# Expert blocks with their weight conversions in another order: one behind each eviction, five behind the last, and the cast of the scatter's indices behind the last eviction

## The chip, the cores and the metric

The kernel runs on one core of a Trainium2 chip. Such a core has five engines that each work through a list of their own: TensorE (PE, matmuls), VectorE (DVE), ScalarE (ACT), GpSimd (POOL) and SyncE (SP, which here issues nearly all transfers). What is compared is the device time of one execution in microseconds (us). Each profile is one execution, with a time stamp for every instruction.

## The reference

Three stages follow each other: attention masked by cluster, a feed-forward layer with a softmax gate on its hidden values, and a layer of eight experts in which each token goes to one expert. The change touches the last stage alone:

```python
expert_idx = np.argmax(logits, axis=1)          # N = 1536 tokens, E = 8 experts, capacity = 384
# token i goes to row pos[i] of expert expert_idx[i], in order, as long as rows are free
h = np.maximum(np.einsum('ecd,edf->ecf', disp, w1), 0.0)    # D = 512, F = 1024
y = np.einsum('ecf,efd->ecd', h, w2)
out[i] = gate_w[i] * y[expert_idx[i], pos[i]]               # zero where no row was free
```

The weights `w1` and `w2` come as 32-bit numbers, 4 MB per expert.

## The kernel before, in words

**How an expert is computed.** Every 32-bit operand is split into two 16-bit numbers, a high part and a low part, and a product is made of three matmuls (high x high, high x low, low x high). For the weights, ScalarE converts to the high part (`ah` for `w1`, `bh` for `w2`, L990) and VectorE computes the low part from the 32-bit number and the high part (`al`, `bl`, L991). An expert's weights come in eight pieces of 0.5 MB: 0 to 3 are `w1`, 4 to 7 are `w2`. SP loads each piece into a staging buffer (`w`, L987) of which the stage has eight, and each buffer can be loaded again when VectorE's conversion has read it.

**A block.** `block(e)` records the work of expert e on its first 256 tokens (in block 0, on its second 128 tokens). The first product (`gemm1`, L1065 to L1067) fills four banks of PSUM with the hidden values, 24 matmuls each. Each bank is evicted by two instructions: ScalarE writes the high part `hh` (L1078) and VectorE the low part `hl` (L1079), which reads `hh` too. Then the second product (`gemm2`, L1084 to L1086) runs through the hidden values once for each 128 tokens, 24 matmuls of 512 columns each; every third one (L1086) reads `hl`. ScalarE scales the result (`yo`, L1089), and GpSimd scatters it to the tokens' rows in DRAM (L1092). The row numbers of the scatter come with the tokens: SP loads them as 32-bit floats (`idf`, L1036) and VectorE casts them to integers (`ids`, L1042). Where an expert has more than 256 tokens, a branch runs `extra` for the rest; this part stands in the program between the first matmuls of the next block.

**What a block does for later ones.** While block e computes, it loads the tokens of expert e + 1 (`cxT`, L1032, and `idf`) and eight pieces of weights: 2 to 7 of expert e + 2 and 0 and 1 of expert e + 3. It converts the eight pieces that the block before has loaded: 2 to 7 of expert e + 1 and 0 and 1 of expert e + 2.

**What sets the order.** Each block is planned by itself. `add` takes for each step its engine, a cost, a due time `at`, and the keys that it reads and writes. `order` sorts the steps by `at` and derives the dependences from the keys in that order; `emit` then plays the steps through on a model of the engines and issues them in the order in which they start there. In the expert stage the due time weighs most in the choice (`MIX` is 0.1). The times of this model are those of the planner and not of the chip; only the order that results goes into the program. The waits between the engines are put in from the real buffers, so a planner's dependence that is missing or one too many changes an order and nothing else.

In the kernel before, the pieces' conversions are due at 5.0, 7.0, 9.0 and so on, two steps (ScalarE's and VectorE's) of a piece together, and none is held back beyond the first eviction (key `("hh", b, 0)`). The cast `ids` is due right behind its load (`at + 0.02`).

Of the kernel before, what the change touches and what calls it, by code (L numbers as in the profile page):

```python
# [25 lines left out]
CAP = 384  # L26
P = 128
# [3 lines left out]
KC, FC = DM // P, DF // P  # L31
# [42 lines left out]
class Plan:  # L74
# [12 lines left out]
    def add(self, eng, cost, at, fn, reads=(), writes=(), data=0.0, lead=1e9, get=None, put=None):  # L87
        if put is not None:
            put.puts += 1
        self.todo.append((eng, cost, at, fn, tuple(reads), tuple(writes), data, lead, get, put))  # L90
# [906 lines left out]
def c_piece(nc, plan, piece, e, i, at, later=None):  # L997

    n = 8 * e + i
    j = n % 3 if n < FIRST else 3 + (n - FIRST) % LATE  # L1000
    cost = dict(sp=0.6, act=0.95, dve=1.14)

    def conv(eng, f, at, reads=()):
        plan.add(eng, cost[eng], at, f, reads=[("cst", j), *reads], writes=[("cw", e, i)])

    def run(eng, f):
        if eng == "sp":
            plan.add(eng, cost[eng], at, f, reads=["turn"], writes=[("cst", j)], data=0.52)
        elif later is None:
            conv(eng, f, at + 6)  # L1010
        else:
            later.append(lambda at, reads: conv(eng, f, at, reads))

    piece(e, i, run)


class Experts:
# [23 lines left out]
        s = slice(a // P, b // P)  # L1041
        self.nc.vector.tensor_copy(out=self.X[e][2][:, s], in_=self.X[e][1][:, s])  # L1042

    def xload(self, e, at, parts):
        add = self.plan.add

        def rows(a, b):
            if e not in self.X:
                self.X[e] = self.tiles(self.xk, e, CAP) if e >= 0 else self.tiles(self.pools["cx0"], e, P)
            self.rows(e, a, b)  # L1050

        for a, b in parts:
            k = (e % 2, b)
            add("sp", 2.7 * (b - a) / CAP, at, lambda a=a, b=b: rows(a, b), reads=["xs", "turn"], writes=[("cxT", k)], data=0.97 * (b - a) / CAP)
        for a, b in parts:
            k = (e % 2, b)
            add("sp", 0.65, at + 0.01, lambda a=a, b=b: self.idf(e, a, b), reads=["xs", ("cxT", k)], writes=[("idf", k)], data=0.06)
            add("dve", 0.07, at + 0.02, lambda a=a, b=b: self.ids(e, a, b), reads=[("idf", k)], writes=[("ids", k)])

    def gemm1(self, o, e, f, j, nb):  # L1060
        nc, w, x = self.nc, self.W[max(e, 0)], self.X[e][0]
# [34 lines left out]
    def block(self, e, start):  # L1096
        add, plan = self.plan.add, self.plan
        b = e % 2
        j0, nb = (1, 1) if e == 0 else (0, 2)
        per = 4 // nb  # L1100
        t = 2.0
        if e == 0:
            self.xload(0, 0.0, [(P, 2 * P), (2 * P, CAP)])
        if e + 1 < E:
            self.xload(e + 1, 1.5, [(0, CAP)])
        last, self.later = self.later, []
        for n, f in enumerate(last):
            f(5.0 + 2.0 * (n // 2), [("hh", b, 0)])
        for n, i in enumerate(range(8 * e + start, min(8 * e + start + 8, 8 * E))):
            c_piece(self.nc, plan, self.piece, i // 8, i % 8, 6.0 + 2.0 * n if e else 1.6 + 0.1 * n, self.later)  # L1110
        kx = [("cxT", (b, 2 * P if e == 0 else CAP))]
        for n in range(FC // per):
            k = Hold()
            for f in range(per):
                def g1(k=k, f=f, n=n):
                    if not (n or f):
                        self.hidden(e, nb)
                    self.gemm1(k.bank[:, f * nb * P : (f + 1) * nb * P], e, per * n + f, j0, nb)

                add("pe", 0.645 * nb, t, g1, reads=kx + [("cw", e, i) for i in range(4)], writes=[k], get=None if f else k)  # L1120
                t += 0.645 * nb
            add("act", 0.48, t, lambda k=k, n=n: self.evac(k.bank, e, n, nb)[0](), reads=[k], writes=[("hh", b, n)])
            add("dve", 0.6, t + 0.01, lambda k=k, n=n: self.evac(k.bank, e, n, nb)[1](),
                reads=[k, ("hh", b, n)], writes=[("hl", b, n)], put=k)
        for i in range(nb):
            k = Hold()
            for f in range(FC):
                add("pe", 0.645, t + 0.02, lambda f=f, k=k, i=i: self.gemm2(k.bank, e, f, i),
                    reads=[("hh", b, f // per), ("hl", b, f // per), ("cw", e, 4 + f // 2)], writes=[k], get=None if f else k)
                t += 0.645  # L1130
            add("act", 0.48, t + 0.02, lambda k=k, i=i: self.scale(k.bank, i), reads=[k], writes=[("yo", i)], put=k)
            add("pool", 1.0, t + 0.03, lambda i=i: self.put(e, j0 + i, i),
                reads=[("yo", i), ("ids", (b, 2 * P if e == 0 else CAP))], data=0.26)
        plan.emit()
# [192 lines left out]
```

## Time and profile before

| | |
|---|---|
| median of three runs | 578.1 us (576.29 to 578.87) |
| the profiled execution | 578.46 us |
| its span in the profile | 576.7 us |
| TensorE busy | 502.8 us (87%) |
| VectorE busy | 414.8 us (72%) |
| ScalarE busy | 365.2 us (63%) |
| GpSimd busy | 276.9 us (48%) |

The expert stage begins at about 396 us. The busy share of an engine is a mean over stages of which each has its own limit, so what a stage is limited by is read from the waits in that stage. A matmul's recorded duration is longer than the time until the next one can start; distances from start to start say more than durations. The third part of expert 2 (`extra`) is run here, inside block 3; in the other blocks the branch is passed over.

### The profile page before, as it was taken

What the parts mean: (1) busy time and instruction counts of PE and PEld (TensorE: products, weight loads), DVE (VectorE), ACT (ScalarE), POOL (GpSimd) and SP (SyncE); (2) the same over time, 40 slices, a digit from 0 to 9 for tenths busy, and PEclk for the clock granted to TensorE, in tenths of its full rate; (3) what the DMA queues carried; (4) which work ended last, traced back from release to release, by engine and by line L of the source; (5) the groups of instructions that cost most, each with busy time, mean ns of one, the idle gap of its engine ahead of it and who ended that gap; (6) DMA issues with size and microseconds to landing.
All of it is one profiled execution on the core that took longest, in us unless ns stands there. A gap on an engine that the chain in (4) does not pass through costs nothing. (4 is left out here: it accounts for less than half of the span.)

```text
span 576.7 us, 13094 instructions
## 1 busy us (share of the span) xinstructions
PE 502.8 (87%) x4945; PEld 325.5 (56%) x4945; DVE 414.8 (72%) x976; ACT 365.2 (63%) x553; POOL 276.9 (48%) x292
## 2 busy tenths in 40 slices
PE   1578898878788888997988999998989999999996
PEld 1356676656565554654554444465746775675672
DVE  7699999999989899997655999961436253753610
ACT  3576897988677898996845889831616162562420
POOL 2167798999978767888742444520000101001001
PEclk9967998999889999999999999999999999999999
DMA  8898777796878799999999687958988456984300
GB/s 247 237 186 226 243 204 215 209 289 158 180 188 184 171 206 156 209 221 196 209 194 237 184 198 196 270 126 178 324 304 233 162 141 234 298 219 160 73 9 17
DMA packets 159340, 113.75 MB, mean 197 GB/s; under 512 B 126560, under 2 KB 135074, under 8 KB 159268
## 3 DMA queue, kind: packets, MB, share of 16 engines
q1 hardware_dynamic: 156660, 106.31, 76.2%
q0 software_dynamic: 2320, 6.32, 3.1%
q8 instruction: 46, 0.75, 0.5%
q14 instruction: 26, 0.21, 0.1%
q10 hardware_dynamic: 288, 0.16, 0.1%
HBM read 51.57 MB, written 17.11 MB: 119 GB/s over the span
## 5 line engine op out<-in xcount | busy, mean ns | idle before, releaser
L408 POOL TENSOR_TENSOR pr<-pf,pr 128x384 f16<-128x384 f32 x168 | 173.6, 1063 | 52.5 <-ACT pr L460 26.2
L1092 POOL DMA_INDIRECT out_dram<-yo,ids x16 | 16.0, 1000 | 160.5 <-ACT yo L1089 131.8
L1065 PE MATMUL psb<-cxT,ah 128*128 128x256 f16 (+1 forms) x288 | 71.8, 261 | 1.7 <-DMA cxT<-xs 1.7
L1067 PE MATMUL psb<-cxT,al 128*128 128x256 f16 (+1 forms) x288 | 71.9, 261 | 0.9 <-PEq L1168 0.3
L1066 PE MATMUL psb<-cxT,ah 128*128 128x256 f16 (+1 forms) x288 | 71.8, 261 | 0.0
L502 DVE TENSOR_REDUCE mm<-psb 128x1 f32<-128x384 f32 x132 | 67.0, 545 | 4.9 <-PE psb L499 4.3
L1079 DVE SCALAR_TENSOR_TENSOR hl<-psb,hh 128x512 f16<-128x512 f32 x32 | 21.8, 685 | 67.2 <-ACT hh L1078 41.8
L536 PE MATMUL psS<-QK 96*128 96x384 f32 x132 | 61.2, 498 | 0.0
L499 PE MATMUL psb<-QK 96*128 96x384 f32 x132 | 46.9, 418 | 14.6 <-DVE mm L502 7.5
L544 ACT ACTIVATE pf<-psS 128x768 f32<-128x768 f32 x66 | 53.2, 806 | 9.5 <-PE psS L536 6.3
L1089 ACT ACTIVATE yo<-psb 128x512 f32<-128x512 f32 x17 | 10.1, 597 | 77.4 <-PE psb L1086 50.0
L544 ACT ACTIVATE pr<-psS 128x768 f16<-128x768 f32 x66 | 52.6, 803 | 8.7 <-PE psS L536 8.5
L1086 PE MATMUL psb<-bh,hl 128*128 128x512 f16 x128 | 48.6, 380 | 4.9 <-DVE hl L1079 4.9
L1084 PE MATMUL psb<-bh,hh 128*128 128x512 f16 x128 | 48.5, 379 | 0.0
L1085 PE MATMUL psb<-bl,hh 128*128 128x512 f16 x128 | 48.5, 379 | 0.0
L535 PE MATMUL psS<-QK 128*128 128x384 f16 x132 | 46.1, 349 | 1.6 <-ACT pr L544 1.0
L557 PE MATMUL psb<-V,pr 128*128 128x65 f16 x396 | 43.7, 196 | 3.9 <-DVE mm L502 3.6
L991 DVE SCALAR_TENSOR_TENSOR al<-w,ah 128x1024 f16<-128x1024 f32 x32 | 38.9, 1244 | 8.2 <-ACT ah L990 8.2
L559 PE MATMUL psb<-V,pr 128*128 128x65 f16 x396 | 43.4, 194 | 1.1 <-POOL pr L408 1.1
L558 PE MATMUL psb<-V,pr 128*128 128x64 f16 x396 | 43.4, 198 | 0.0
L557 PEld LDWEIGHTS <-pr 128*128 128x128 f16 x396 | 37.3, 98 | 7.4 <-issue 2.6
L558 PEld LDWEIGHTS <-pr 128*128 128x128 f16 x396 | 37.7, 99 | 5.4 <-issue 4.4
(193 smaller groups left out, 1561.2 us busy)
## 6 DMA issues: line engine op xcount, KB each, us to landing
w<-in_w_dram SPq DMA_DIRECT2D x64, 512.0 KB
xs<-X SPq DMA_DIRECT2D x12, 516.0 KB
QK<-hr SPq DMA_DIRECT2D x16, 384.0 KB
QK<-hl SPq DMA_DIRECT2D x32, 192.0 KB
x<-in_qkT_dram SPq DMA_DIRECT2D x7, 768.0 KB
lT<-in_w_in_dram SPq DMA_DIRECT2D x8, 512.0 KB
lT<-in_w_out_dram SPq DMA_DIRECT2D x8, 512.0 KB
v<-in_vP_dram SPq DMA_DIRECT2D x8, 384.0 KB
```

Of the source, the lines that this page charges most:

```text
L408: nc.gpsimd.tensor_tensor(out=out[:, i], in0=a[:, i], in1=b[:, i], op=ALU.subtract)
L502: add("dve", 0.465, at(c - 9.9 + 0.25 * g), lambda c=c, g=g, w=w: nc.vector.tensor_reduce(out=m2[mm][:, c, g : g + 1], in_=w.bank[:, :384] ...
L536: nc.tensor.matmul(o, k1[:, ks], q1[:, qs], start=False, stop=True)
L544: add("act", 0.691, at(k + 0.5), lambda dst=dst, kb=kb: nc.scalar.activation(dst, ps[kb][:, :, :384], AF.Exp, scale=SC), reads=[kb], write ...
L557: nc.tensor.matmul(A, ph[ub][:, c, qs], v[:, j, c, 0:65], start=(c == 0), stop=False)
L558: nc.tensor.matmul(A[:, :64], ph[ub][:, c, qs], v[:, j, c, 65:129], start=False, stop=False)
L1065: nc.tensor.matmul(o, w["ah"][:, c, fs], x[:, 0, c, ts], start=(c == 0), stop=False)
L1066: nc.tensor.matmul(o, w["ah"][:, c, fs], x[:, 1, c, ts], start=False, stop=False)
L1067: nc.tensor.matmul(o, w["al"][:, c, fs], x[:, 0, c, ts], start=False, stop=(c == KC - 1))
L1084: nc.tensor.matmul(y, hh[:, f, i], w["bh"][:, f], start=(f == 0), stop=False)
L1085: nc.tensor.matmul(y, hh[:, f, i], w["bl"][:, f], start=False, stop=False)
L1086: nc.tensor.matmul(y, hl[:, f, i], w["bh"][:, f], start=False, stop=(f == FC - 1))
```

## The change

It gives other due times and other keys to two kinds of steps; no instruction is added or removed.

- The k-th piece's conversion (k from 0) is now due and held behind the eviction of bank g = min(k, 3) (in block 0, which has two banks: min(k, 1)): the first conversion behind the first eviction, the second behind the second, the third behind the third, and the other five behind the fourth.
- The cast `ids` is now due behind the block's last bank and is held behind that bank's `hh` (the last one: `FC // per - 1`).

```diff
-    def xload(self, e, at, parts):
+    def xload(self, e, at, parts, late=()):
...
-            add("dve", 0.07, at + 0.02, lambda a=a, b=b: self.ids(e, a, b), reads=[("idf", k)], writes=[("ids", k)])
+            add("dve", 0.07, late[0] if late else at + 0.02, lambda a=a, b=b: self.ids(e, a, b), reads=[("idf", k), *late[1:]], writes=[("ids", k)])
...
+        late = (2.4 + 0.645 * nb * FC, ("hh", b, FC // per - 1))
         if e == 0:
-            self.xload(0, 0.0, [(P, 2 * P), (2 * P, CAP)])
+            self.xload(0, 0.0, [(P, 2 * P), (2 * P, CAP)], late)
         if e + 1 < E:
-            self.xload(e + 1, 1.5, [(0, CAP)])
+            self.xload(e + 1, 1.5, [(0, CAP)], late)
         last, self.later = self.later, []
         for n, f in enumerate(last):
-            f(5.0 + 2.0 * (n // 2), [("hh", b, 0)])
+            g = min(n // 2, FC // per - 1)
+            f(2.3 + 0.645 * nb * per * (g + 1) + 1.2 * (n // 2 - g), [("hh", b, g)])
```

The program up to the expert stage is the same instruction for instruction. TensorE's list is the same throughout. On VectorE the list of block 1 reads as follows before; `hl_1` is an eviction, `al` and `bl` are conversions with the piece's number in `w_2` to `w_7`, and `ids` is the cast.

```order
L1079 SCALAR_TENSOR_TENSOR hl_1_6336<-psb_4711,hh_1_6335 128x512
L991 SCALAR_TENSOR_TENSOR al_5453<-w_2_6097,ah_5452 128x1024
L991 SCALAR_TENSOR_TENSOR al_5453<-w_3_6112,ah_5452 128x1024
L991 SCALAR_TENSOR_TENSOR bl_5455<-w_4_6127,bh_5454 128x1024
L1079 SCALAR_TENSOR_TENSOR hl_1_6336<-psb_75,hh_1_6335 128x512
L991 SCALAR_TENSOR_TENSOR bl_5455<-w_5_6141,bh_5454 128x1024
L1079 SCALAR_TENSOR_TENSOR hl_1_6336<-psb_73,hh_1_6335 128x512
L991 SCALAR_TENSOR_TENSOR bl_5455<-w_6_6155,bh_5454 128x1024
L1042 CAST ids_6351<-idf_6350 128x3
L991 SCALAR_TENSOR_TENSOR bl_5455<-w_7_6168,bh_5454 128x1024
L1079 SCALAR_TENSOR_TENSOR hl_1_6336<-psb_4710,hh_1_6335 128x512
```

Six conversions and the cast stand ahead of the last eviction. In the changed kernel the same stretch reads:

```order
L1079 SCALAR_TENSOR_TENSOR hl_1_6336<-psb_4711,hh_1_6335 128x512
L991 SCALAR_TENSOR_TENSOR al_5453<-w_2_6097,ah_5452 128x1024
L1079 SCALAR_TENSOR_TENSOR hl_1_6336<-psb_75,hh_1_6335 128x512
L991 SCALAR_TENSOR_TENSOR al_5453<-w_3_6112,ah_5452 128x1024
L1079 SCALAR_TENSOR_TENSOR hl_1_6336<-psb_73,hh_1_6335 128x512
L991 SCALAR_TENSOR_TENSOR bl_5455<-w_4_6127,bh_5454 128x1024
L1079 SCALAR_TENSOR_TENSOR hl_1_6336<-psb_4710,hh_1_6335 128x512
L1042 CAST ids_6351<-idf_6350 128x3
L991 SCALAR_TENSOR_TENSOR bl_5455<-w_5_6141,bh_5454 128x1024
L991 SCALAR_TENSOR_TENSOR bl_5455<-w_6_6155,bh_5454 128x1024
L991 SCALAR_TENSOR_TENSOR bl_5455<-w_7_6166,bh_5454 128x1024
```

Three conversions stand ahead of the last eviction, the cast behind it, and five conversions behind the cast. ScalarE's list moves in the same way: `hh` and a conversion in turn, and behind the fourth `hh` five conversions, then the scaling of the outputs. On SP, before, the list of block 2 begins so; `cxT` and `idf` are the tokens and the row numbers of expert 3, and `w_2` to `w_6` the pieces of expert 4.

```order
L1032 DMA_TRANSPOSE cxT_6687<-xs 128x8x384
L987 DMA w_2_6746<-in_w_dram 128x1024
L987 DMA w_3_6763<-in_w_dram 128x1024
L1036 DMA idf_6688<-xs 128x3x1
L987 DMA w_4_6780<-in_w_dram 128x2x512
L987 DMA w_5_6798<-in_w_dram 128x2x512
L987 DMA w_6_6812<-in_w_dram 128x2x512
```

And in the changed kernel:

```order
L1032 DMA_TRANSPOSE cxT_6687<-xs 128x8x384
L987 DMA w_4_6715<-in_w_dram 128x2x512
L987 DMA w_5_6718<-in_w_dram 128x2x512
L987 DMA w_2_6748<-in_w_dram 128x1024
L1036 DMA idf_6688<-xs 128x3x1
L987 DMA w_3_6779<-in_w_dram 128x1024
L987 DMA w_6_6827<-in_w_dram 128x2x512
```

Pieces 4 and 5 have moved ahead of 2 and 3, and `idf` stands behind three loads instead of two. In both kernels the k-th load of a block takes the buffer that the k-th conversion of the block frees, and waits for that conversion on VectorE. The fourth load (`w_3`) so waits for the fourth conversion, which in the changed kernel stands behind the cast, and the cast waits for `idf`.

## Rows read from the trace of the kernel before

**Rows 1.** The page: TensorE's busy time, and the chain that ended last.

```profile
PE 502.8 (87%) x4945; PEld 325.5 (56%) x4945; DVE 414.8 (72%) x976; ACT 365.2 (63%) x553; POOL 276.9 (48%) x292
...
issue 7%; DMA 3%; DVE 0%; ACT 0%; POOLq 0%; POOL 0%
```

**Rows 2.** TensorE's waits from 390 us: us in total, times, longest.

```profile
PE psb L1086 <- DVE hl L1079: 4.9, 4, 2.4
PE psb L1065 <- DMA cxT<-xs: 1.7, 1, 1.7
```

**Rows 3.** Timeline of TensorE: start us, us, engine, line, operation, count, [idle before].

```profile
421.76 0.38 PE L1085 MATMUL psb<-bl,hh 128*128 128x512 f16 x1
424.58 0.39 PE L1086 MATMUL psb<-bh,hl 128*128 128x512 f16 x1 [2.44 <-DVE hl L1079]
...
447.34 0.39 PE L1086 MATMUL psb<-bh,hl 128*128 128x512 f16 x1 [1.43 <-DVE hl L1079]
...
479.47 0.39 PE L1086 MATMUL psb<-bh,hl 128*128 128x512 f16 x1 [0.58 <-DVE hl L1079]
...
500.42 0.38 PE L1085 MATMUL psb<-bl,hh 128*128 128x512 f16 x1
500.82 0.39 PE L1086 MATMUL psb<-bh,hl 128*128 128x512 f16 x1
...
522.58 0.39 PE L1086 MATMUL psb<-bh,hl 128*128 128x512 f16 x1 [0.43 <-DVE hl L1079]
```

**Rows 4.** Timeline of ScalarE, blocks 1, 2, 6 and 7.

```profile
409.69 0.60 ACT L1078 ACTIVATE hh<-psb 128x512 f16<-128x512 f32 x1 [2.02 <-PE psb L1067]
410.41 2.00 ACT L990 ACTIVATE ah<-w 128x1024 f16<-128x1024 f32 x2
412.32 1.04 ACT L990 ACTIVATE bh<-w 128x1024 f16<-128x1024 f32 x1
...
433.45 0.60 ACT L1078 ACTIVATE hh<-psb 128x512 f16<-128x512 f32 x1 [2.02 <-PE psb L1067]
...
531.46 0.60 ACT L1078 ACTIVATE hh<-psb 128x512 f16<-128x512 f32 x1 [1.97 <-PE psb L1067]
...
552.61 0.60 ACT L1078 ACTIVATE hh<-psb 128x512 f16<-128x512 f32 x1 [1.97 <-PE psb L1067]
...
560.78 0.60 ACT L1078 ACTIVATE hh<-psb 128x512 f16<-128x512 f32 x1 [2.02 <-PE psb L1067]
566.01 0.60 ACT L1089 ACTIVATE yo<-psb 128x512 f32<-128x512 f32 x1 [4.63 <-PE psb L1086]
```

**Rows 5.** Timeline of VectorE, block 1.

```profile
411.88 0.69 DVE L1079 SCALAR_TENSOR_TENSOR hl<-psb,hh 128x512 f16<-128x512 f32 x1 [0.58 <-DVEq L1168]
412.49 2.35 DVE L991 SCALAR_TENSOR_TENSOR al<-w,ah 128x1024 f16<-128x1024 f32 x2
414.76 1.22 DVE L991 SCALAR_TENSOR_TENSOR bl<-w,bh 128x1024 f16<-128x1024 f32 x1
...
418.23 1.21 DVE L991 SCALAR_TENSOR_TENSOR bl<-w,bh 128x1024 f16<-128x1024 f32 x1
422.59 0.17 DVE L1042 CAST ids<-idf 128x3 int32<-128x3 f32 x1 [3.16 <-DMA idf<-xs]
...
423.84 0.68 DVE L1079 SCALAR_TENSOR_TENSOR hl<-psb,hh 128x512 f16<-128x512 f32 x1
```

**Rows 6.** Timeline of SP, block 3.

```profile
470.12 1.46 SPq L987 DMA_DIRECT2D w<-in_w_dram  x2
```

**Rows 7.** Stretches: engines' busy us, TensorE's clock, DMA share, GB/s.

```profile
409.90:431.20 21.30, 18.71 (x124) 11.71 (x123) 11.92 (x14) 10.48 (x14) 1.07 (x1) 1.00 1.01 303
431.20:454.00 22.80, 21.22 (x147) 13.98 (x145) 11.85 (x13) 10.91 (x15) 2.03 (x2) 1.00 0.84 243
486.10:507.40 21.30, 21.12 (x146) 13.89 (x144) 11.85 (x13) 10.87 (x15) 2.03 (x2) 1.00 0.84 250
470.00:471.00 1.00, 1.00 (x11) 0.90 (x10) 1.00 (x2) 1.00 (x2) 0.00 (x0) 1.00 0.06 19
```

## The prediction

> **What bounds the kernel now.** Start with the page's first part: the span is 576.7 us and TensorE (PE) is busy 502.8 us of it, more than any other engine [rows 1]. The chain that ended last does not help here. It covers about a tenth of the span, and what it holds is the last results' way out and time that it calls "issue" [rows 1]. So I read TensorE's own waits over the experts' stretch, from 390 us to the end. The largest is that of the second product (L1086) for `hl`, the low part of the hidden values, which VectorE (DVE) writes when it evicts a bank: 4.9 us in four waits, the longest 2.4 us [rows 2]. The wait for the first expert's tokens, 1.7 us, is not touched by the change.
>
> The timeline of TensorE shows where these waits lie: in the second product of an expert block, always at a matmul that reads `hl` [rows 3]. The idle time in brackets understates the loss, because a matmul is recorded with 0.38 us while the next one starts sooner. What counts is from start to start. In block 7, which has no stall, the last eviction on ScalarE (ACT) starts at 560.78 us and the scaling of the first output at 566.01 us, with 24 matmuls of the second product between: 5.23 / 24 = 0.22 us each [rows 4]. In rows 3 the bracket and the 0.38 us of the matmul before make that distance: 2.44 + 0.38 = 2.82 us in block 1, and likewise 1.81 us in block 2, 0.96 us in block 3 and 0.81 us in block 5; in block 4, where no bracket stands, it is 500.82 - 500.42 = 0.40 us. Less 0.22 us each they lose 2.60 + 1.59 + 0.74 + 0.59 + 0.18 = 5.70 us. A second count agrees for block 1: from the first eviction of block 1 to that of block 2 pass 433.45 - 409.69 = 23.76 us, in block 6, which has no stall, 552.61 - 531.46 = 21.15 us; the difference, 2.61 us, is block 1's loss [rows 4].
>
> Why is `hl` late? VectorE works in the order of its list. In block 1 it ends a conversion that started at 418.23 us and took 1.21 us, and then stands 3.16 us for the cast of the scatter's indices, whose `idf` lands late [rows 5]. Behind the cast come one more conversion and only then the block's last eviction, at 423.84 us; it ends at 424.52 us and TensorE starts again at 424.58 us [rows 3, 5]. The bank was full long before: by block 7's distance (560.78 - 552.61 = 8.17 us) the last `hh` of block 1 can start at 409.69 + 8.17 = 417.86 us [rows 4]. So the eviction comes about five microseconds after it could.
>
> **Part 1, the cast behind the last eviction.** No instruction is added or dropped. The 3.16 us wait (and the like in the other blocks) moves behind the fourth `hl`, where no eviction stands behind it. What stands behind it now are five conversions, and the loads that wait for them; that is priced below.
>
> **Part 2, one conversion behind each eviction.** Take block 1. VectorE's first eviction starts at 411.88 us in both kernels: it follows a branch and the cast of the block before, which do not move. With 0.69 us for an eviction [rows 5] and (414.76 - 412.49) / 2 = 1.14 us from one conversion's start to the next [rows 5]: `al` 412.5 to 413.7, eviction 2 behind its `hh` to 414.4, `al` to 415.5, eviction 3 (its `hh` starts one bank, 8.17 / 3 = 2.7 us, before the last and is ready at 415.8) to 416.5, `bl` (its `bh` behind that `hh` on ScalarE, ready at 416.7) to 417.8, eviction 4 when its `hh` (417.86 + 0.6) is ready, 418.5 to 419.2 us. TensorE would come to the first matmul that needs it at 421.76 + 0.22 = 421.98 us [rows 3]. That leaves 2.8 us in hand in the block with the latest start; the other blocks start earlier against their own TensorE, so their stalls go too. ScalarE has the room: between two evictions 2.7 us apart stand 0.6 us of eviction and one conversion of (412.32 - 410.41) / 2 = 0.96 us [rows 4].
>
> What is late next? On ScalarE five conversions now stand between the last eviction and the scaling of the first output: 417.86 + 0.5 + 5 x 0.96 = 423.2 us, and the output's bank is full 5.23 us after the last eviction's start, at 423.1 us. A scaling late by 0.1 us holds only its store and a bank that is wanted a block later; I cost it at nothing, and 0.1 us at most per block in the store. In block 7, the last, there are no conversions, so the end of the kernel keeps its shape.
>
> **Part 3, the loads on SP.** Each weight load of a block waits until a conversion of the same block has freed a staging buffer, so the loads follow the conversions. `idf` is now queued behind three loads instead of two, and the third of these waits for the third conversion. So `idf` lands about one load later, some 1.5 us (17.9 us of transfers in a block, less the tokens, over eight loads, gives under 2 us each), the cast follows, and the last five loads start only behind the cast. The transfers run dry in between: 0.17 us of cast, 1.22 us of conversion [rows 5], and the time from a load's issue to moving bytes; the load issued into an empty queue at 470.12 us left the stretch from 470 to 471 us at a share of 0.06, so about 1.1 us [rows 6, 7]. A block's own transfers take 0.84 x 21.3 = 17.9 us to 0.84 x 22.8 = 19.2 us [rows 7]. The loop from cast to cast is then 17.9 + 2.5 = 20.4 us to 19.2 + 2.5 = 21.7 us, against a block of 21.15 us: it gains 0.8 us or loses 0.5 us per block. How late may it get? The cast of block 1 stood 422.59 - 409.69 = 12.9 us after the first eviction's start [rows 4, 5]; add 1.5 us for the third load, and five conversions end at 14.4 + 5.9 = 20.3 us. TensorE needs the last `hl` at 421.98 - 409.69 = 12.3 us into the next block, and four evictions with three conversions take 4 x 0.69 + 3 x 1.14 = 6.2 us, so VectorE may come free as late as 21.15 + 12.3 - 6.2 = 27.2 us: 6.9 us in hand. A drift of 0.5 us over the three links from block 3 to block 6 does not use it up. I cost part 3 at 0. A gain is not in it, since no wait of TensorE for weights stands in its list [rows 2]; the other bound is rival C.
>
> On the dry queue the Trainium skill has a harder price: its page DMA: Bandwidth & Descriptors, section "Anatomy of one DMA — SWDGE (gpsimd) path", gives every DMA a fixed cost of about 2 us, most of it until the last byte is confirmed. The row above shows 1.1 us up to the first bytes and not the confirmation. By the page the loop would be an estimated 0.9 us longer and drift by up to 1.4 us per block, which speaks against the change, but three links of it still end short of the margin.
>
> **The sum.** 5.70 us off, nothing added. The profiled execution took 578.46 us, 1.8 us more than its span, and that rest stays: 578.46 - 5.70 = 572.76, so 572.7 us. The median of the runs before is 578.1 us, 0.36 us below the profiled one, and the runs spread from 576.29 to 578.87 us; from the median it would be 572.4 us. I keep 572.7.
>
> **The rivals.** B, half of it stays: the conversions that now stand ahead of the second to fourth eviction find their weights not landed, since the pieces 2 and 3 are now the third and fourth load of a block, the latter behind the cast. Then `al` waits in front of an eviction. For: these loads move later by several microseconds. Against: they land some 6 us before the next block begins. It would give back about half, 2.85 us: 575.6 us. C, slower: the loop of part 3 becomes the bound. Its place is the cast on VectorE, its point a loop above 21.15 + 6.9 / 3 = 23.5 us. The stretch of block 4 moved 250 GB/s x 21.3 us = 5.3 MB [rows 7]; if the transfers, cut in two by the dry queue, ran at 200 GB/s, the block's would take 26.6 us and the loop 29 us, 8 us a block too long. Two such links, 3 to 5, cost 16 - 6.9 = 9 us, one link from 1 to 2 another 1 us: 572.7 + 10 = 583 us. Against: 1.01 of share at 303 GB/s in block 1's stretch, with a backlog, shows that the rate rises when more is queued [rows 7]. D, no change: TensorE's next wait, which this trace cannot show while the stall is there, takes the time back: 578 us. For it I find no row; the granted clock is 1.00 in every stretch of rows 7, with the stalls in it, so no clock is lost or to be won by their going.
>
> **Chances and range.** Forecast 0.82, B 0.08, C 0.06, D 0.04. The runs before lie within 0.45% of each other, and about 0.5% is what a measurement can tell from no change, 2.9 us: below 575.2 us is faster. Of the forecast's 0.82 I give 0.03 to a measurement that misses that line; with B and D that is 0.15 for no change, 0.79 are faster; C is slower, 0.06. Faster 0.79, same 0.15, slower 0.06. The range is 571.2 to 576.3 us: the forecast's own spread of 1.5 us below, and on the other side up to B.
>
> **What would show it.** Right: TensorE's waits for `hl` are gone or under 0.5 us in sum; from one block's first eviction on ScalarE to the next pass 21.2 us in blocks 1, 2, 4, 5 and 6 alike; the cast still waits for `idf`, longer than before, with nothing of TensorE behind it; the last loads of a block are issued later. Wrong: `al` waiting in front of an eviction (B), VectorE's first eviction of a block late behind `al` conversions of the block before (C), or equal block lengths with the time lost at another place (D).

## The result: 571.8 us, ratio 0.9879, and the profile after

The changed kernel took 571.82 us (median of four executions, 568.89 to 572.98), the kernel before 578.39 us on the same chip. The ratio is 0.9879, 95% interval 0.9841 to 0.9918. The profiled execution took 571.86 us, 6.60 us less than the profiled one before.

TensorE's waits from 390 us on, read as in [rows 2] (us in total, times, longest). The wait for `hl` is not in the list any more:

```profile
PE psb L1065 <- DMA cxT<-xs: 0.6, 1, 0.6
```

The timeline of ScalarE, which answers to [rows 4]; the first eviction of blocks 1, 2, 6 and 7, and of block 1 the last eviction and the first scaling too:

```profile
408.68 0.60 ACT L1078 ACTIVATE hh<-psb 128x512 f16<-128x512 f32 x1 [2.02 <-PE psb L1067]
...
416.85 0.60 ACT L1078 ACTIVATE hh<-psb 128x512 f16<-128x512 f32 x1 [1.08 <-PE psb L1067]
...
422.08 0.60 ACT L1089 ACTIVATE yo<-psb 128x512 f32<-128x512 f32 x1
...
429.83 0.60 ACT L1078 ACTIVATE hh<-psb 128x512 f16<-128x512 f32 x1 [2.02 <-PE psb L1067]
...
524.66 0.60 ACT L1078 ACTIVATE hh<-psb 128x512 f16<-128x512 f32 x1 [1.97 <-PE psb L1067]
...
545.82 0.60 ACT L1078 ACTIVATE hh<-psb 128x512 f16<-128x512 f32 x1 [1.97 <-PE psb L1067]
```

Block 1 now takes 429.83 - 408.68 = 21.15 us instead of 23.76 us [rows 4], as long as block 6 (545.82 - 524.66 = 21.16 us), which had no stall before either. The scaling starts 422.08 - 416.85 = 5.23 us behind the last eviction, the distance of block 7 before [rows 4]: the five conversions between the two do not delay it.

The timeline of VectorE, which answers to [rows 5]: block 1 with the cast of block 0 ahead of it, the first eviction of block 2, and the casts of blocks 2 to 5:

```profile
412.89 0.17 DVE L1042 CAST ids<-idf 128x3 int32<-128x3 f32 x1 [8.95 <-DMA idf<-xs]
413.64 0.69 DVE L1079 SCALAR_TENSOR_TENSOR hl<-psb,hh 128x512 f16<-128x512 f32 x1 [0.58 <-DVEq L1170]
414.25 1.22 DVE L991 SCALAR_TENSOR_TENSOR al<-w,ah 128x1024 f16<-128x1024 f32 x1
415.38 0.68 DVE L1079 SCALAR_TENSOR_TENSOR hl<-psb,hh 128x512 f16<-128x512 f32 x1
...
418.85 0.68 DVE L1079 SCALAR_TENSOR_TENSOR hl<-psb,hh 128x512 f16<-128x512 f32 x1
425.40 0.17 DVE L1042 CAST ids<-idf 128x3 int32<-128x3 f32 x1 [5.86 <-DMA idf<-xs]
425.50 3.50 DVE L991 SCALAR_TENSOR_TENSOR bl<-w,bh 128x1024 f16<-128x1024 f32 x3
428.92 2.35 DVE L991 SCALAR_TENSOR_TENSOR al<-w,ah 128x1024 f16<-128x1024 f32 x2
431.42 0.69 DVE L1079 SCALAR_TENSOR_TENSOR hl<-psb,hh 128x512 f16<-128x512 f32 x1
...
446.46 0.17 DVE L1042 CAST ids<-idf 128x3 int32<-128x3 f32 x1 [7.14 <-DMA idf<-xs]
...
474.10 0.17 DVE L1042 CAST ids<-idf 128x3 int32<-128x3 f32 x1 [3.40 <-DMA idf<-xs]
...
495.21 0.17 DVE L1042 CAST ids<-idf 128x3 int32<-128x3 f32 x1 [3.36 <-DMA idf<-xs]
...
516.78 0.17 DVE L1042 CAST ids<-idf 128x3 int32<-128x3 f32 x1 [3.77 <-DMA idf<-xs]
```

The cast waits longer than before, 5.86 us instead of 3.16 us [rows 5], but the block's last eviction (418.85 us) is already done. The stretches, as in [rows 7] (busy us of TensorE, its weight loads, VectorE, ScalarE and GpSimd, then TensorE's granted clock, DMA share and GB/s), block 1 and then single microseconds around the cast of block 4:

```profile
408.70:429.80 21.10, 20.95 (x146) 13.98 (x144) 10.46 (x13) 11.14 (x14) 2.68 (x2) 1.00 0.89 271
...
494.00:495.00 1.00, 1.00 (x6) 0.49 (x5) 0.00 (x0) 1.00 (x2) 0.00 (x0) 1.00 0.04 8
495.00:496.00 1.00, 1.00 (x7) 0.44 (x5) 0.79 (x2) 1.00 (x2) 0.00 (x0) 1.00 0.00 0
496.00:497.00 1.00, 1.00 (x6) 0.44 (x5) 1.00 (x2) 0.36 (x1) 0.36 (x1) 1.00 0.00 0
497.00:498.00 1.00, 1.00 (x6) 0.49 (x5) 1.00 (x2) 0.00 (x0) 1.00 (x1) 1.00 0.31 106
```

TensorE is busy in 20.95 of 21.10 us of block 1. The transfers do run dry around the cast, as part 3 said, and TensorE (1.00 of each microsecond) takes no notice.

### The profile page after: what moved, and what is told of

It is laid out like the page before. It is cut to its first block, busy times and chain, and to the rows that moved or that the text cites. A ratio compares the mean times of both kernels' runs of the same rounds, so it can differ in the third digit from the quotient of the medians.

```text
span 570.1 us, 13098 instructions
## 1 busy us (share of the span) xinstructions
PE 500.6 (88%) x4945; PEld 325.1 (57%) x4945; DVE 415.2 (73%) x976; ACT 366.1 (64%) x553; POOL 280.3 (49%) x292
## 5 line engine op out<-in xcount | busy, mean ns | idle before, releaser
L1092 POOL DMA_INDIRECT out_dram<-yo,ids x16 | 19.0, 1188 | 150.8 <-ACT yo L1089 106.2
L1078 ACT ACTIVATE hh<-psb 128x512 f16<-128x512 f32 x32 | 19.1, 597 | 49.0 <-PE psb L1067 49.0
L991 DVE SCALAR_TENSOR_TENSOR al<-w,ah 128x1024 f16<-128x1024 f32 x32 | 40.5, 1278 | 7.8 <-ACT ah L990 7.5
L557 PEld LDWEIGHTS <-pr 128*128 128x128 f16 x396 | 37.5, 98 | 7.3 <-issue 2.5
```

Source lines behind the costliest of these rows:

```text
L557: nc.tensor.matmul(A, ph[ub][:, c, qs], v[:, j, c, 0:65], start=(c == 0), stop=False)
```

## The experiments

Eight kernels were run, two of them twice. The totals of one kernel mostly differ by 0.7 to 1.3% between its executions, so the second measure, read from the one profile of each row, is the stretch from block 0's first eviction on ScalarE to the last scaling, with the block lengths in it (first eviction to first eviction). The start of block 0 alone differs between the ten profiles from 396.17 to 401.94 us; that lies ahead of all that is changed here. Block 6 is 21.15 or 21.16 us in all of them.

| kernel | block 0 | 1 | 2 | 3 | 4 | 5 | stretch us | ratio to before, 95% interval |
|---|---|---|---|---|---|---|---|---|
| before | 10.48 | 23.76 | 22.76 | 32.14 | 21.35 | 21.76 | 171.98 | 1 |
| changed | 10.48 | 21.15 | 21.15 | 31.38 | 21.15 | 21.15 | 166.19 | 0.9879 (0.9841 to 0.9918) |
| conversions only | 14.34 | 21.15 | 21.15 | 31.38 | 21.15 | 21.15 | 170.05 | 0.9921 (0.9888 to 0.9954) |
| cast only | 10.48 | 24.71 | 21.15 | 31.38 | 21.15 | 21.15 | 169.75 | 0.9902 (0.9868 to 0.9936) |
| before, early indices | 11.44 | 21.15 | 21.15 | 31.38 | 21.15 | 21.15 | 167.15 | 0.9916 (0.9880 to 0.9952) |
| cast ahead | 11.39 | 28.34 | 22.11 | 32.19 | 22.08 | 21.90 | 177.74 | 1.0076 (1.0043 to 1.0109) |
| changed, again | 10.48 | 21.15 | 21.15 | 31.38 | 21.15 | 21.15 | 166.19 | 0.9898 (0.9864 to 0.9933) |
| conversions only, again | 11.79 | 21.15 | 21.15 | 31.38 | 21.15 | 21.15 | 167.50 | 0.9907 (0.9869 to 0.9944) |
| changed, early indices | 10.49 | 21.14 | 21.15 | 31.38 | 21.15 | 21.15 | 166.19 | 0.9868 (0.9822 to 0.9914) |
| cast only, early indices | 10.48 | 21.14 | 21.15 | 31.39 | 21.14 | 21.15 | 166.18 | 0.9860 (0.9818 to 0.9903) |

Each ratio is to the kernel before as it was timed beside that kernel. The totals tell before, cast ahead, and the rest apart. Among the rest only the stretch does, and it speaks for one execution: the two profiles of conversions only differ by 2.55 us in block 0.

**Theory:** an eviction that stands on VectorE's list behind the cast waits for a late `idf`, and TensorE waits for the eviction. **Rival:** it is the number of conversions ahead of the eviction. A second rival: the loads, which now pass through the cast, set the length of a block.

**Conversions only.** The changed kernel without `late` in the two calls of `xload`, run twice:

```diff
-            self.xload(0, 0.0, [(P, 2 * P), (2 * P, CAP)], late)
+            self.xload(0, 0.0, [(P, 2 * P), (2 * P, CAP)])
-            self.xload(e + 1, 1.5, [(0, CAP)], late)
+            self.xload(e + 1, 1.5, [(0, CAP)])
```

> The conversions' new places alone; the cast of the next expert's indices keeps its old due time. In the planned order the cast then falls behind the block's last eviction by itself in every block but block 0. Theory (what counts is whether VectorE meets the cast, or six conversions, ahead of the block's last eviction): as the changed kernel, 571 to 573 us, blocks 1 to 6 without a wait of TensorE for hl. Rival (the cast's own move is what gives the time): near the kernel before, 576 to 578 us.

Blocks 1 to 6 are as in the changed kernel, by the theory; the cast stands behind their last eviction here too, so in them this kernel does not tell the two moves apart. The median of 575.54 us missed the expected 571 to 573 us and lies next to the rival's range. Block 0 was not priced there, and in the profile it lost 3.86 us: its own two casts stand ahead of its last eviction. TensorE in block 0 of this kernel (start, us, ..., [idle before]):

```profile
401.46 0.38 PE L1085 MATMUL psb<-bl,hh 128*128 128x512 f16 x1
403.85 0.39 PE L1086 MATMUL psb<-bh,hl 128*128 128x512 f16 x1 [2.01 <-DVE hl L1079]
404.07 0.38 PE L1084 MATMUL psb<-bh,hh 128*128 128x512 f16 x1
...
405.21 0.63 PE L1086 MATMUL psb<-bh,hl 128*128 128x512 f16 x1
405.64 0.63 PE L1084 MATMUL psb<-bh,hh 128*128 128x512 f16 x1
```

Its stretches there (the last three columns are TensorE's granted clock, DMA share, GB/s):

```profile
402.00:404.00 2.00, 0.15 (x1) 0.12 (x2) 0.91 (x3) 0.00 (x0) 0.00 (x0) 1.00 1.03 388
404.00:406.00 2.00, 2.00 (x8) 0.78 (x7) 0.00 (x0) 0.00 (x0) 0.00 (x0) 0.77 1.00 303
406.00:408.00 2.00, 2.00 (x9) 1.04 (x8) 0.00 (x0) 0.60 (x1) 0.00 (x0) 0.50 1.04 389
```

The stall itself is 403.85 - 401.46 - 0.22 = 2.17 us. The other 1.7 us come from the granted clock, which fell to 0.50 about a microsecond after the stall and stayed there to about 408.4 us: from 405.21 us on, matmuls start 0.43 us apart instead of 0.22.

The kernel before has the same list on VectorE in block 0 and lost nothing there in its one profile (10.48 us). VectorE in block 0 of the kernel before:

```profile
403.02 0.35 DVE L1042 CAST ids<-idf 128x1 int32<-128x1 f32 x2 [2.43 <-DMA idf<-xs]
403.28 0.68 DVE L1079 SCALAR_TENSOR_TENSOR hl<-psb,hh 128x512 f16<-128x512 f32 x1
```

And of conversions only:

```profile
402.82 0.37 DVE L1042 CAST ids<-idf 128x1 int32<-128x1 f32 x2 [5.27 <-DMA idf<-xs]
```

The casts came 403.02 - 399.21 = 3.81 us after the block's first eviction before, and 402.82 - 396.17 = 6.65 us here; TensorE needs the last `hl` 401.46 + 0.22 - 396.17 = 5.51 us after it. VectorE has no conversion in block 0. So what block 0 loses goes by when its `idf` lands in an execution, and not by the conversions' move. The loads of the two `idf` were issued 0.37 us ahead of the block's first eviction before (398.84 us) and 2.14 us behind it here (398.31 us). TensorE had stood 1.7 us for the first tokens in the profile before [rows 2] and 0.5 us here, which fits a block that began later against its loads. Whether the kernel before loses time in block 0 in other executions is not known from one profile.

> The conversions' new places alone, a second profile. Theory (the cast's own move matters in block 0 alone, where two casts stand ahead of its last eviction): blocks 1 to 6 as the changed kernel, block 0 up to 4 us longer than the changed kernel's 10.5 us, by how late idf lands; by the median 1 to 4 us slower than the changed kernel. Rival (the 3.9 us of block 0 were a chance of one execution): median within 1 us of the changed kernel.

The second profile has the same stall, smaller, and its clock stays at 1.00: block 0 is 1.31 us longer than in the changed kernel. TensorE in block 0 of the second profile:

```profile
405.59 0.39 PE L1086 MATMUL psb<-bh,hl 128*128 128x512 f16 x1 [1.14 <-DVE hl L1079]
```

The two medians, 573.65 us here and 572.37 us for the changed kernel beside it, lie as the theory has them, but their intervals overlap; the stretch shows the cast's own due time to be worth 1.3 to 3.9 us in block 0 of these two executions, and nothing in the later blocks.

**Cast only.** The changed kernel with the conversions' old due times:

```diff
-            g = min(n // 2, FC // per - 1)
-            f(2.3 + 0.645 * nb * per * (g + 1) + 1.2 * (n // 2 - g), [("hh", b, g)])
+            f(5.0 + 2.0 * (n // 2), [("hh", b, 0)])
```

> The cast behind the last eviction alone; the conversions keep their old places, six of the seven ahead of the block's last eviction. Theory (the cast's wait is the cause): VectorE reaches the last eviction about 6 x 1.14 + 2 x 0.6 = 8.0 to 8.6 us after its first one. TensorE needs it 12.3 us after the first eviction of ScalarE; VectorE's first stood 2.2 us (before) to 5.0 us (changed) behind that in block 1. So blocks 2 to 5 lose nothing and block 1 loses 0 to 2 us: 572 to 574.5 us. Rival (the conversions ahead of the eviction are the cause): most of the 5.7 us stays, 576 to 578 us.

The median, 573.09 us, is as expected. In the profile, which is of the longest of the six executions (578.18 us), blocks 2 to 5 lose nothing, as expected, and block 1 lost 3.56 us, against 0 to 2. VectorE there:

```profile
417.33 0.17 DVE L1042 CAST ids<-idf 128x3 int32<-128x3 f32 x1 [10.16 <-DMA idf<-xs]
418.08 0.69 DVE L1079 SCALAR_TENSOR_TENSOR hl<-psb,hh 128x512 f16<-128x512 f32 x1 [0.58 <-DVEq L1169]
...
424.43 2.35 DVE L991 SCALAR_TENSOR_TENSOR bl<-w,bh 128x1024 f16<-128x1024 f32 x2
426.69 0.69 DVE L1079 SCALAR_TENSOR_TENSOR hl<-psb,hh 128x512 f16<-128x512 f32 x1
```

From the first eviction to the last pass 8.61 us, as reckoned. But the first one stands 418.08 - 411.60 = 6.48 us behind ScalarE's (411.60 us is 401.12 plus block 0's 10.48), because the cast of block 0, which is ahead of it on VectorE's list, had to wait for its `idf` until 417.33 us. The last eviction ends at 427.38 us, 411.60 + 12.3 = 423.9 us was wanted. By its size this fits the rival too; the next two kernels decide.

**Early indices.** In `xload`, the `idf` of every expert from 1 to 7 is issued ahead of its tokens (the expectations name experts 1 to 3; the condition `e > 0` holds for all seven):

```diff
+            if e > 0:
+                self.idf(e, a, b)
...
-            add("sp", 0.65, at + 0.01, lambda a=a, b=b: self.idf(e, a, b), reads=["xs", ("cxT", k)], writes=[("idf", k)], data=0.06)
+            add("sp", 0.65, at + 0.01, lambda a=a, b=b: None if e > 0 else self.idf(e, a, b), reads=["xs", ("cxT", k)], writes=[("idf", k)], data=0.06)
```

First this alone, added to the kernel before:

> The kernel before, with VectorE's order as it was (cast and six conversions ahead of the last eviction), but the load of the indices of experts 1 to 3 is issued ahead of these experts' tokens, so that it has landed long before the cast. Theory (the late landing of idf is what the cast stood for): the cast waits under 0.2 us, the last eviction of block 1 comes 3.2 us earlier, the 5.7 us of stalls go all but 0 to 1 us: 572 to 574 us. Rival (it is the list's length, not the wait): the stalls stay at over 3 us in sum, 575 to 578 us.

VectorE in block 1 of that kernel, whose list is that of the kernel before:

```profile
421.01 0.17 DVE L1042 CAST ids<-idf 128x3 int32<-128x3 f32 x1
421.08 1.22 DVE L991 SCALAR_TENSOR_TENSOR bl<-w,bh 128x1024 f16<-128x1024 f32 x1
422.21 0.69 DVE L1081 SCALAR_TENSOR_TENSOR hl<-psb,hh 128x512 f16<-128x512 f32 x1
```

The cast and six conversions still stand ahead of the last eviction, the cast waits for nothing, and all five stalls are gone. The rival falls. The median, 574.93 us, is 0.9 us above the expected range. The stretch shows 0.96 us lost in block 0; this is a new loss, since the kernel before lost nothing there in its profile. VectorE in block 0 of this kernel:

```profile
406.26 0.36 DVE L1042 CAST ids<-idf 128x1 int32<-128x1 f32 x2 [4.05 <-DMA idf<-xs]
```

Block 0's own two casts, whose `idf` is not loaded earlier, came 406.26 - 400.83 = 5.43 us after its first eviction, against 3.81 us before; expert 1's `idf` now stands ahead of theirs on SP. Then the same with the cast alone moved:

> The cast behind the last eviction, conversions in their old places, and the indices of experts 1 to 3 loaded early. Theory (what the cast alone lost in block 1, 3.56 us, came from block 0's late cast ahead of block 1's first eviction, with six conversions behind it): VectorE's first eviction of block 1 stands 0.6 to 1 us behind ScalarE's, the last ends at about 10 us of the 12.3 us, no block loses anything: 166.2 us from block 0's first eviction to the last output. Rival (six conversions ahead of the last eviction are too many by themselves): 1.5 us or more stay in block 1.

VectorE's first and last eviction in block 1 (ScalarE's first is at 398.38 + 10.48 = 408.86 us):

```profile
409.49 0.69 DVE L1081 SCALAR_TENSOR_TENSOR hl<-psb,hh 128x512 f16<-128x512 f32 x1 [5.80 <-ACTq L1171]
...
418.68 0.68 DVE L1081 SCALAR_TENSOR_TENSOR hl<-psb,hh 128x512 f16<-128x512 f32 x1
```

The last eviction ends 419.36 - 408.86 = 10.5 us into the block, in time for the 12.3 us, and the 3.56 us are gone. So cast only lost them through block 0's late cast, not through the six conversions by themselves.

**Cast ahead.** The changed kernel with the cast ahead of the last eviction again:

```diff
-        late = (2.4 + 0.645 * nb * FC, ("hh", b, FC // per - 1))
+        late = (2.0 + 0.645 * nb * FC, ("hh", b, FC // per - 2))
...
-                reads=[k, ("hh", b, n)], writes=[("hl", b, n)], put=k)
+                reads=[k, ("hh", b, n)] + [("ids", ((e + 1) % 2, CAP))] * (n == 3 and e + 1 < E), writes=[("hl", b, n)], put=k)
```

> The changed kernel with its conversions and its loads on SP as they are, but the cast ahead of the block's last eviction again. Theory (a wait ahead of the eviction is TensorE's wait): idf lands 12.9 to 16.7 us after the block's first eviction, the last eviction ends 0.8 us behind it, TensorE needs it at 12.3 us: 5.2 us lost in block 1, 5.1 in block 2, about 1.4 in blocks 3 and 4, 1.8 in block 5, some 15 us in all, 584 to 588 us, slower than before the change by 6 to 10 us. Rival (once the conversions are spread, the place of the cast doesn't matter): 571 to 573 us.

VectorE in block 1:

```profile
429.20 0.17 DVE L1042 CAST ids<-idf 128x3 int32<-128x3 f32 x1 [6.64 <-DMA idf<-xs]
429.28 0.68 DVE L1079 SCALAR_TENSOR_TENSOR hl<-psb,hh 128x512 f16<-128x512 f32 x1
```

TensorE there:

```profile
425.62 0.27 PE L1065 MATMUL psb<-cxT,ah 128*128 128x256 f16 x1
430.02 0.61 PE L1086 MATMUL psb<-bh,hl 128*128 128x512 f16 x1 [4.13 <-DVE hl L1079]
430.42 0.63 PE L1084 MATMUL psb<-bh,hh 128*128 128x512 f16 x1
```

And its stretches:

```profile
428.00:430.00 2.00, 0.00 (x0) 0.00 (x0) 0.80 (x3) 0.00 (x0) 0.00 (x0) 0.77 0.16 23
430.00:432.00 2.00, 1.98 (x5) 0.73 (x6) 2.00 (x2) 0.01 (x1) 0.00 (x0) 0.50 0.00 0
```

The stalls are back, 177.74 - 166.19 = 11.55 us, and the kernel is slower than before the change (583.78 us beside 579.30 us). The size was off: expected were some 15 us and 584 to 588 us. Block 1 lost 7.19 us, of which 430.02 - 425.62 = 4.4 us, less the 0.1 us of one short matmul, are the stall, and the rest a granted clock of 0.50 that began within it. Block 2 lost 0.96 us, not 5.1: its cast came 12.5 us after the block's first eviction and not 16.7; the transfers had gone on while block 1 stood (share 1.06 from 426 to 428 us). Block 0 lost 0.91 us, since its two casts are ahead of its last eviction again.

**The changed kernel again, and with early indices.**

> The changed kernel once more, timed beside the next three. From block 0's first eviction to the last output 166.2 us as before; what differs between two profiles of it lies ahead of block 0. The cast of block 0's indices lands 3 to 6 us after block 1's first eviction, and block 1 loses nothing as long as that is under 5.6 us (4.2 us and 1.4 us in hand in the first profile).

> The changed kernel with the indices of experts 1 to 3 loaded ahead of these experts' tokens, so that the cast never waits and the last five loads of a block start without it. Theory (behind the last eviction the cast's wait and the loads behind it hold nobody up): from block 0's first eviction to the last output 166.2 us, the same as the changed kernel, within 0.3%. Rival (the loop of loads through the cast costs something): faster by over 1 us.

In the changed kernel's two profiles the block lengths agree to 0.01 us. In the second profile of the changed kernel block 0's cast landed at 414.64 us, 4.2 us after block 1's first eviction (399.97 + 10.48), as in the first. With early indices the cast of block 4 does not wait and the last five loads go out earlier. VectorE in block 4:

```profile
491.02 0.16 DVE L1042 CAST ids<-idf 128x3 int32<-128x3 f32 x1
```

And SP's last loads of block 4:

```profile
492.61 4.90 SPq L987 DMA_DIRECT2D w<-in_w_dram  x5
```

SP in block 4 of the changed kernel:

```profile
491.13 0.43 SPq L1036 DMA_DIRECT2D idf<-xs  x1
496.57 4.88 SPq L987 DMA_DIRECT2D w<-in_w_dram  x5
```

From the block's first eviction to these loads pass 14.2 us in the changed kernel (496.57 - 482.36) and 11.0 us here (492.61 - 481.61); both stretches are 166.19 us. The cast's wait and the loads behind it hold nobody up, and the second rival falls. No kernel of the eight beats the changed one by more than the intervals can tell, and the stretch is the same in the three best, to 0.01 us.

## Why the prediction was right

**The sum.** Forecast were 5.70 us off the expert blocks; the stretch shrank by 171.98 - 166.19 = 5.79 us, block by block 2.61, 1.61, 0.76, 0.20 and 0.61 us where the count from start to start gave 2.60, 1.59, 0.74, 0.18 and 0.59. The profiled time fell by 6.60 us: 5.79, and 1.01 us because block 0 began earlier (398.20 instead of 399.21 us), less 0.20 us behind the last scaling. The 1.01 us are no work of the change: they lie ahead of it, and the second profile of the changed kernel began block 0 at 399.97 us. So 572.7 us was forecast and 571.8 us measured.

**Part 1 and part 2.** The mechanism holds, but the parts don't divide as the prediction told it. With the conversions moved, the planner put the cast behind the last eviction by itself in every block but block 0. The cast's own due time adds block 0, where conversions only lost 1.3 to 3.9 us; the prediction did not name it, and none of the 5.79 us is from there, since the kernel before lost nothing in block 0 in its profile.

**One step was wrong in size.** "VectorE's first eviction starts at 411.88 us in both kernels", behind a cast of the block before that does not move. That cast keeps its place in the list but did come later. In the kernel before it is:

```profile
411.13 0.17 DVE L1042 CAST ids<-idf 128x3 int32<-128x3 f32 x1 [7.17 <-DMA idf<-xs]
```

It came 4.2 us after block 1's first eviction instead of 1.4 us (412.89 - 408.68; 411.13 - 409.69 before). So the last eviction ended at 419.53 us against 408.68 + 12.3 = 421.0 us, 1.4 us in hand instead of 2.8. The step held because only three conversions stand between first and last eviction; with six of them a cast that was later still (417.33 - 411.60 = 5.7 us) cost the cast-only kernel 3.56 us. Spreading the conversions is what pays for block 0's cast. That the step held is in part luck: by the 1.4 us left at 4.2 us, a cast at 5.7 us would have used up all that the changed kernel has in hand (an estimate; no run shows it). Why that `idf` lands later is not settled: its load was issued 5.9 us after block 0's first eviction instead of 3.6 us, 1.0 us of that because block 0 began earlier.

**Part 3.** Forecast was a loop of 20.4 to 21.7 us from cast to cast. It is 446.46 - 425.40 = 21.06 us from block 1 to 2, 495.21 - 474.10 = 21.11 us from 3 to 4 and 516.78 - 495.21 = 21.57 us from 4 to 5, a drift of 0.4 us at most. The start of the loop was mis-sized: block 1's cast was forecast 14.4 us after the block's first eviction and came at 425.40 - 408.68 = 16.7 us. Its five conversions ended at 428.92 + 2.35 - 408.68 = 22.6 us instead of 20.3, which left 4.6 us of the forecast's 6.9 us in hand. The dry stretch was underrated: forecast 2.5 us, measured 4 x 1 - (0.04 + 0.31) = 3.65 us from 494 to 498 us. The missing microsecond lies ahead of the cast: from 494 us on almost nothing moves (share 0.04), yet the cast starts at 495.21 us. For a DMA that GpSimd issues, the Trainium skill (DMA: Bandwidth & Descriptors, "Anatomy of one DMA — SWDGE (gpsimd) path") puts most of a fixed cost of about 2 us into the time until the last byte is confirmed. These loads are issued by SyncE, so the section is not about them; the trace is near it all the same, since the 2.5 us plus the prediction's estimated 0.9 us make 3.4 us, and 3.65 us were measured. The loop itself stayed within the forecast.

**The rivals.** B: neither ScalarE's nor VectorE's list shows a conversion waiting for a weight. C: no loop came near its 23.5 us. Its sign did show once: VectorE's first eviction of block 2, at 431.42 us, stands right behind two `al` conversions, 1.6 us after ScalarE's (429.83 us). It cost nothing, for block 2 took 21.15 us. D: TensorE's list shows no new wait. The scaling on ScalarE was priced at up to 0.1 us late and is not late at all.

## What to carry to other kernels

On an engine that works in order, an instruction that waits for a small late transfer belongs behind the last instruction that a busier engine waits for; it doesn't matter that it takes 0.17 us itself. Read what such a wait costs from start to start on the engine that bounds the time, and look at the block before as well: its waiting instruction stands ahead of the next block's first one. Loading the small thing earlier cured the same stalls here without any reordering of the evictions (blocks 1 to 5 of early indices), and made the order matter less.

## What the runs showed of the hardware that was not expected

In two of the ten profiles a stall of TensorE cost 1.7 to 1.8 times its length. After an idle time of 2.01 us (conversions only) the granted clock was 0.50, the 1.2 GHz level of its two, from about 405 to 408.4 us, and a stall of 2.17 us cost 3.86; in one of 4.13 us (cast ahead) it fell before TensorE went on, and was 0.50 up to about 435.9 us; a stall of 4.3 us cost 7.19. In the other eight profiles the clock is 1.00 in every microsecond from 390 to 566 us. But the longest idle time before the change, 2.44 us [rows 3], left it at 1.00, and so did 1.14 us in the second profile of conversions only. The length of the idle time alone doesn't tell which it will be; what else decides was not tried.

A load of 1.5 KB (`idf`) behind three weight loads took 495.21 - 491.13 = 4.1 us from its issue to the start of the cast in block 4, and 6.0 us in block 1 (425.40 - 419.38). In block 4 the first of the three was issued 3.5 us ahead of it, in block 1 only 1.6 us.
